# Routing one group of tiles a tile later, and giving small work to GpSimd, in a fused attention and expert kernel

## The chip, the cores and the metric

The kernel runs on one core of a Trainium2 chip. The metric is the device time of one execution in microseconds (us); lower is better. A core has five engines with instruction queues of their own: TensorE (PE in the profile; PEld is its loading of stationary operands), VectorE (DVE), ScalarE (ACT), GpSimd (POOL) and SyncE (SP), which here only issues transfers. Each queue runs in order, and engines wait for one another by semaphores. GpSimd issues the indirect transfers (scatters of rows to computed addresses).

## The reference

```python
def _attn_ref(q, k, v, omega):           # q, k, v: 8 x 8 x 576 x 64; omega: 128 x 64
    ...
    q_p, k_p = (phi(q_s), phi(k_s))      # phi: exp(h - max h) of h = x @ omega.T - |x|^2 / 2
    kv = np.einsum('bhsm,bhsd->bhmd', k_p, v)
    z = np.sum(k_p, axis=2)
    num = np.einsum('bhsm,bhmd->bhsd', q_p, kv)
    den = np.einsum('bhsm,bhm->bhs', q_p, z)[..., None] + 1e-06
    return (num / den).astype(np.float32)

def _moe_ref(x, expert_emb, tau, w1, w2):   # x: 4608 x 512, 8 experts, w1: 512 x 1024, w2: 1024 x 512
    xn = x / (np.linalg.norm(x, axis=-1, keepdims=True) + 1e-06)
    en = expert_emb / (np.linalg.norm(expert_emb, axis=-1, keepdims=True) + 1e-06)
    logits = xn @ en.T / tau
    expert_idx = np.argmax(logits, axis=1)
    ...                                      # gate_w: softmax weight of the chosen expert
    for e in range(E):
        mask = expert_idx == e
        ...
        h = np.maximum(x[mask] @ w1[e], 0.0)
        out[mask] = gate_w[mask, None] * (h @ w2[e])
    return out.astype(np.float32)
```

Linear attention with random features gives 4608 rows of 512; each row is routed to the one expert with the highest logit, and its result is weighted with the softmax weight of that expert.

## The kernel before

**Attention.** The 4608 tokens are 36 tiles of 128, nine to a pair of batch entries. One loop runs over `i` from 0 to 44. In pass `i` the key features of tile `i` are made and added into the key-value sums, and the query features of tile `iq = i - 7` (LAG is 7) are made: VectorE finds the maxima (nmk, nmq, L368), ScalarE takes the exponentials (ftk, ftq, L377), TensorE transposes (L451), ScalarE and VectorE copy (qp, L456 and L458), TensorE multiplies with the key-value sums (L471), giving `nuu` in PSUM. `num_out` (L476 to L493) divides by the denominator on VectorE, and writes the tile's row block `xr` (L490) and its logits (L486).

**Routing.** Every three tiles (a group, G is 3, 12 groups) `routed(g)` runs as a generator whose steps are put at chosen places of later passes by `plan`, with four kinds of place: `spare` and `mid` between the pieces of a pass, `ends` behind it, `behind` after the loop. Its steps: the sum of the logits over heads, on GpSimd in three operations (L510 to L512) or, for the last three groups (`fast`), on VectorE in one (L506); the maximum and the difference (L514, L515); a copy of the logits into xr on GpSimd (L518); the choice `sel` (L519 to L521); the counting of earlier rows with the same expert on TensorE (L526, L528); row numbers `base`, `pos` (L533 to L547, GpSimd, or VectorE for the last three groups); the cast of `pos` to integers `posi` on VectorE (L553); and then three scatters of the tiles' rows to `xs` in device memory, one by one (L559). For groups in `DRAINS` GpSimd's queue is drained ahead of the first scatter (L557).

**The first expert.** After group 5 (GPICK) `pick_first` (L565 to L580) chooses the expert with the most rows so far. Its weights are loaded in eight quarters from pass 29 on and split into a high and a low part: `first_split` rounds on ScalarE or VectorE, `first_rest` (L603) subtracts on GpSimd in four pieces of 128x256. From pass 36 on the generator `first_steps` gives TensorE two tiles of that expert's work between the pieces of attention, with the norms of their rows from a square root by integer and float steps (`root`, L145 and L146 on VectorE, then 13 operations on GpSimd, L148 to L156).

**Expert steps.** After the loop come the padding rows (`pad`), the table of steps, and 36 steps `t` from 2 to 37 (`ends` is 37). Each multiplies one tile of 128 rows with a pair of weight matrices, as three products of high and low parts (L280): the hidden layer, then the down product of an earlier step (`u = t - 2`). Weights come by quarters; `split` rounds them on VectorE (L230) and subtracts on GpSimd (L235) in four pieces, in one piece for the last two steps. The hidden rows are transposed by transfers on SyncE (L1050), put together on VectorE (L1062) and split (L1078, L1082). `x_of(t + 3)` loads rows into a ring of six tiles (L183), `scaled` multiplies by the gate (L287), `store` scatters the rows to the output (L310). In a step from 6 on the order is: scaling, w1 split, store, w2 split, hidden product, transposes, down product, x load of step t + 3.

**The end** (L1232 to L1250). The down product of step 36, scaling of step 35, the w2 split, the store of 35, the down product of step 37, scaling and store of step 36, one more w2 split, a DRAIN of GpSimd's queue, the last row half on ScalarE (L1247) and half on VectorE (L1248), and its store. A loop for further steps follows, which runs only when the table needs more than 38.

TensorE's and GpSimd's orders in the attention stage are as written by hand; so are VectorE's and ScalarE's in the loop.

## Time and profile before

| | |
|---|---|
| time, median of 3 runs | 646.91 us (646.56 to 648.96) |
| profiled execution: time | 647.41 us |
| its span, first to last instruction | 645.8 us |
| mean granted TensorE clock | 0.994 of full |
| TensorE busy | 627.1 us (97%) |
| VectorE busy | 498.0 us (77%) |
| ScalarE busy | 431.4 us (67%) |
| GpSimd busy | 423.7 us (66%) |

The times are of whole executions; the rows below are of the profiled one, whose span leaves 1.6 us of its time outside. The attention loop ends near 224 us, the expert steps fill the rest.

### The profile page before, as it was taken

How to read it: one execution, taken by the hardware profiler on the slowest of the kernel's cores; microseconds unless marked ns; L12 is line 12 of the kernel's file. 1: busy time of each engine (PE TensorE's matmuls, PEld its weight loads, DVE VectorE, ACT ScalarE, POOL GpSimd, SP SyncE). 2: the span in 40 equal slices, each digit the busy share in tenths (PEclk: the TensorE clock that was granted, in tenths of full speed). 3: DMA queues.
4: the chain of work that ended last, by engine and by line, in shares of the span. 5: the costliest groups of instructions: out<-in, count | busy, mean ns of one | idle time of the engine just before them, and what ended most of it. 6: DMA issues, size and time to landing. Idle time of an engine off the chain costs nothing.

```text
span 645.8 us, 19034 instructions
## 1 busy us (share of the span) xinstructions
PE 627.1 (97%) x6289; PEld 535.3 (83%) x6290; DVE 498.0 (77%) x926; ACT 431.4 (67%) x1102; POOL 423.7 (66%) x585
## 2 busy tenths in 40 slices
PE   8999999989989999999999999999999999999995
PEld 8899989988977788888888888888888888888884
DVE  4788898899889855687788787787878786878861
ACT  5898898888996426655757575757566656675630
POOL 1212343444888244668878887879897978698864
PEclk9999999999999999999999999999999999999998
DMA  7655665767862167958888888797888786879731
GB/s 250 186 166 167 207 209 180 225 199 272 289 211 101 69 214 295 261 160 247 215 220 206 231 226 211 195 246 200 223 213 233 205 216 205 227 205 219 218 103 45
DMA packets 142238, 131.92 MB, mean 204 GB/s; under 512 B 106742, under 2 KB 106870, under 8 KB 142144
## 3 DMA queue, kind: packets, MB, share of 16 engines
q1 hardware_dynamic: 135520, 109.70, 60.9%
q0 software_dynamic: 6480, 20.91, 9.4%
q8 instruction: 57, 0.93, 0.6%
q14 instruction: 37, 0.30, 0.1%
q10 hardware_dynamic: 144, 0.07, 0.0%
HBM read 83.78 MB, written 21.97 MB: 164 GB/s over the span
## 4 chain that ended last, share of the span: by engine, by line
PE 88%; ACT 4%; DVE 4%; issue 2%; POOL 1%; DMA 1%; POOLq 0%; SPq 0%; DVEq 0%; ACTq 0%
PE pb L280 31%; PE po L280 30%; PE pb L364 10%; PE kva L395 5%; PE nuu L471 5%; PE nuu L451 2%; PE fs_o L280 2%; ACT ftk L377 2%; ACT ftq L377 1%; PE pb L262 1%; PE fs_a L280 1%; DMA kt<-kT 1%; PE nuu L395 1%; DVE xr L490 1%; DVE nmq L368 1%
## 5 line engine op out<-in xcount | busy, mean ns | idle before, releaser
L235 POOL TENSOR_TENSOR w2l<-raww,w2h 128x256 f32 (+1 forms) x130 | 144.1, 1108 | 12.3 <-DVE w2h L230 3.9
L235 POOL TENSOR_TENSOR w1l<-raww,w1h 128x256 f32 (+1 forms) x130 | 122.6, 943 | 44.7 <-DVE w1h L230 34.5
L280 PE MATMUL po<-w2h,hh 128*128 (+1 forms) x288 | 112.4, 390 | 0.4 <-POOL w2l L235 0.4
L280 PE MATMUL po<-w2h,hl 128*128 (+1 forms) x288 | 112.2, 390 | 0.0
L280 PE MATMUL po<-w2l,hh 128*128 (+1 forms) x288 | 112.1, 389 | 0.0
L280 PE MATMUL pb<-w1h,xh 128*128 (+1 forms) x280 | 109.5, 391 | 0.0
L280 PE MATMUL pb<-w1h,xl 128*128 (+1 forms) x280 | 109.0, 389 | 0.0
L280 PE MATMUL pb<-w1l,xh 128*128 (+1 forms) x280 | 109.0, 389 | 0.0
L1044 DVE COPY pl<-pb 128x512 uint16<-128x512 uint16 x68 | 46.7, 689 | 60.0 <-ACT pl L1040 59.7
L377 ACT ACTIVATE ftk<-pb,nmk 128x128 f32<-128x128 f32 x288 | 80.1, 438 | 6.8 <-DVE nmk L368 6.7
L377 ACT ACTIVATE ftq<-pb,nmq 128x128 f32<-128x128 f32 x288 | 79.9, 404 | 3.3 <-DVE nmq L368 3.0
L1040 ACT ACTIVATE pl<-pb 128x512 uint16<-128x512 uint16 x68 | 39.4, 584 | 63.0 <-PE pb L280 32.9
L1062 DVE COPY wd<-t 128x1024 uint16<-128x1024 uint16 x68 | 65.8, 969 | 1.5 <-DMA t<-pl 1.5
L1078 ACT ACTIVATE hh<-wd 128x1024 fp32r<-128x1024 f32 x34 | 36.1, 1062 | 45.6 <-DVE wd L1062 40.0
L280 PEld LDWEIGHTS po<-w2h,hh 128*128 128x128 f32 x288 | 54.1, 188 | 11.9 <-POOL w2l L235 0.8
L280 PEld LDWEIGHTS po<-w2h,hl 128*128 128x128 f32 x288 | 54.0, 188 | 11.6 <-DVE hl L1082 0.3
L280 PEld LDWEIGHTS po<-w2l,hh 128*128 128x128 f32 x288 | 54.0, 187 | 11.2
L280 PEld LDWEIGHTS pb<-w1l,xh 128*128 128x128 f32 x280 | 52.7, 188 | 10.9
L280 PEld LDWEIGHTS pb<-w1h,xl 128*128 128x128 f32 x280 | 52.6, 188 | 11.0
L280 PEld LDWEIGHTS pb<-w1h,xh 128*128 128x128 f32 x280 | 52.5, 187 | 10.7
L1082 DVE SCALAR_TENSOR_TENSOR hl<-wd,hh 128x1024 fp32r<-128x1024 f32 x34 | 55.2, 1622 | 6.6 <-ACT hh L1078 6.2
L559 POOL DMA_INDIRECT xs<-xr,posi x36 | 36.4, 1012 | 28.5 <-DVE qp L458 8.2
(333 smaller groups left out, 1242.5 us busy)
## 6 DMA issues: line engine op xcount, KB each, us to landing
raww<-w1q SPq DMA_DIRECT2D x38, 512.0 KB, 4.0
raww<-w2q SPq DMA_DIRECT2D x38, 512.0 KB, 4.8
kt<-kT SPq DMA_DIRECT2D x36, 256.0 KB, 3.7
qt<-qT SPq DMA_DIRECT2D x36, 256.0 KB, 3.5
xgp<-xs SPq DMA_DIRECT2D x20, 260.5 KB, 2.8
xg<-xs SPq DMA_DIRECT2D x18, 260.5 KB, 2.7
rf<-w1q SPq DMA_DIRECT2D x4, 512.0 KB, 3.6
rf<-w2q SPq DMA_DIRECT2D x4, 512.0 KB, 5.6
```

Source lines behind the costliest of these rows:

```text
L235: ils.append(nc.gpsimd.tensor_tensor(at(l, dp)[:, c], raw[:, c], at(h, dp)[:, c].bitcast(F32), op=ALU.subtract))
L280: done.append(nc.tensor.matmul(dst, x[:, c * P : (c + 1) * P], ws.rearrange("p o f -> p (o f)"), start=(begin and i == 0 and k == 0), stop ...
L364: nc.tensor.matmul(st["pj" + w, i, a][:, c, :], st[w, i][r, c, :], om[r, :], start=True, stop=True)
L377: nc.scalar.activation(ft[:, h, :], pj[:, h, :], AF.Exp, bias=nm[:, h : h + 1])
L395: nc.tensor.matmul(acc[c : c + 64, h, :], ft[:, h, c : c + 64], vt[:, 2 * h + a, :], start=begin and h == 0, stop=u == 4 + 4 * b and h == 3,)
L471: nc.tensor.matmul(pn[a][s * D : s * D + D, h, :], st["qp", i, s][:, 2 * h + a, :], kvs[sb, int(u > 4 - s)][:, 4 * a + h, :], start=True, ...
L559: w = nc.gpsimd.indirect_dma_start(out=xs, out_offset=bass.IndirectOffsetOnAxis(ap=posi[:, j : j + 1], axis=0), in_=xr, in_offset=None, bo ...
L1040: nc.scalar.activation(planes[1][:, o : o + 512], halved(src)[:, :, 1], AF.Copy)
L1044: nc.vector.tensor_copy(planes[0][:, o : o + 512], halved(src)[:, :, 0])
L1062: nc.vector.tensor_copy(to, src)
L1078: nc.scalar.activation(hh, wd[:, 0:F], AF.Relu)
L1082: nc.vector.scalar_tensor_tensor(hl, wd[:, 0:F], 0.0, hh.bitcast(F32), op0=ALU.max, op1=ALU.subtract)
```

## The change

- `posi` is cast on GpSimd for groups 0 to 8, on VectorE for the last three as before.
- `pick_first` makes three operations on VectorE and ten on GpSimd, with a constant `pickc` made at the start.
- The root for the first expert's rows is asked for after three columns of its first product in place of before the first.
- Group 10 (the last but one) sums its logits on GpSimd, and its steps are placed about a pass later.
- Each scatter waits for the latest `num_out`, and the scatters of groups 8 and 9 are placed a pass later, one a pass.
- DRAINs at groups 10 and 11 and at step NQ go; new ones stand before the pads, after the first expert's work and in the last step. Those at groups 3 and 6 wait for the latest `num_out`.
- In the expert steps the store stands ahead of the w1 split, and from step 6 on the x load of step t + 3 ahead of the hidden product.
- At the end the w2 splits of the last two steps are subtracted on VectorE, the first of them ahead of the scaling, and the last row is scaled on ScalarE in one piece.

```diff
-DRAINS = (3, 6, 10, 11)
+DRAINS = (3, 6)
...
+    pickc = const.tile([P, E], F32, name="pickc")
+    nc.gpsimd.tensor_scalar(pickc, iote, -float(REG * E + 1), 0.0, op0=ALU.mult, op1=ALU.add)
...
             piece = F if t is None or t >= NSTAT - 2 else PIECE
+            eng, d = (nc.vector, dv) if wn == "w2" and t is not None and t >= NSTAT - 2 else (nc.gpsimd, dp)
             for c in range(0, F, piece):
                 c = slice(c, c + piece)
-                ils.append(nc.gpsimd.tensor_tensor(at(l, dp)[:, c], raw[:, c], at(h, dp)[:, c].bitcast(F32), op=ALU.subtract))
+                ils.append(eng.tensor_tensor(at(l, d)[:, c], raw[:, c], at(h, d)[:, c].bitcast(F32), op=ALU.subtract))
...
-            nc.vector.tensor_tensor(
+            st["out"] = nc.vector.tensor_tensor(
                 xr[:, 0:DM].rearrange("p (h a d) -> p a h d", a=2, d=D),
...
-            if fast:
+            pt = nc.gpsimd.tensor_tensor
+            if fast and g != NTILE // G - 2:
                 nc.vector.tensor_reduce(raw, lg.rearrange("p g h e -> p g e h"), axis=AX.X, op=ALU.add)
...
-            nc.vector.tensor_copy(posi, pos[:, :, 0])
+            (nc.vector if fast else nc.gpsimd).tensor_copy(posi, pos[:, :, 0])
             for j in range(G):
                 yield
                 if j == 0 and g in DRAINS:
-                    nc.gpsimd.drain()
+                    tc.add_manual_dep(nc.gpsimd.drain().ins, st["out"].ins.name, sync, reason="idle behind the last scatter")
...
+                tc.add_manual_dep(w.ins, st["out"].ins.name, sync, reason="one scatter a tile")
                 written(w)
...
         def pick_first():

+            pt, ts = nc.gpsimd.tensor_tensor, nc.gpsimd.tensor_scalar
             cnt = small.tile([P, E], F32, name="cnt0", tag="cnt")
-            nc.vector.scalar_tensor_tensor(cnt, iote, -float(REG), run, op0=ALU.mult, op1=ALU.add)
             m = small.tile([P, 1], F32, name="m0", tag="m0")
+            nc.vector.scalar_tensor_tensor(cnt, run, float(E), pickc, op0=ALU.mult, op1=ALU.add)
             nc.vector.tensor_reduce(m, cnt, axis=AX.X, op=ALU.max)
-            nc.vector.tensor_scalar(cnt, cnt, m, None, op0=ALU.is_ge)
-            nc.vector.tensor_tensor(cnt, cnt, iotm, op=ALU.mult)
-            nc.vector.tensor_reduce(m, cnt, axis=AX.X, op=ALU.min)
+            nc.vector.tensor_scalar(isf, cnt, m, None, op0=ALU.is_ge)
             yield
-            nc.vector.tensor_scalar(first, m, float(E), None, op0=ALU.add)
+            pt(cnt, isf, iote, op=ALU.mult)
+            pt(cnt[:, 0:4], cnt[:, 0:4], cnt[:, 4:8], op=ALU.add)
+            pt(cnt[:, 0:2], cnt[:, 0:2], cnt[:, 2:4], op=ALU.add)
+            pt(first, cnt[:, 0:1], cnt[:, 1:2], op=ALU.add)
             for t in range(NPRE + 1):
-                nc.vector.tensor_scalar(firsti[:, t : t + 1], first, float(REG), float(t * P), op0=ALU.mult, op1=ALU.add)
-            nc.vector.tensor_copy(firsti[:, NPRE + 1 :], first)
-            nc.vector.tensor_scalar(isf, iote, first, None, op0=ALU.is_equal)
-            nc.vector.scalar_tensor_tensor(keyc, isf, float(2 * E * N), iote, op0=ALU.mult, op1=ALU.subtract)
+                ts(firsti[:, t : t + 1], first, float(REG), float(t * P), op0=ALU.mult, op1=ALU.add)
+            nc.gpsimd.tensor_copy(firsti[:, NPRE + 1 :], first)
+            ts(keyc, isf, float(2 * E * N), 0.0, op0=ALU.mult, op1=ALU.add)
+            pt(keyc, keyc, iote, op=ALU.subtract)
...
+            pa = new("a00", "kv0")
+            yield from up(0, 0, range(3), pa)
             nrm = root(gp, n2, NPRE, "p", nc.gpsimd)
-            yield from up(0, 0, range(4), new("a00", "kv0"))
+            yield from up(0, 0, [3], pa)
...
+                elif g == NTILE // G - 2:
+                    plan = [(ends, i), (ends, i + 1), (ends, i + 1), (spare, i + 2, 0), (mid, i + 2, 0), (mid, i + 2, 1)]
+                    plan += [(ends, i + 2), (ends, i + 3), (ends, i + 3)]
                 elif i >= NTILE:
                     plan = [(ends, i)] * 3 + [(spare, i + 1, 0), (mid, i + 1, 0), (mid, i + 1, 1)]
-                    plan += [(ends, i + 1 + k) for k in range(3)]
+                    plan += [(ends, i + 2 + k) for k in range(3)]
...
                 if NTILE - 3 < i < NTILE:
-                    plan[-3:] = [(ends, i + 3), (ends, i + 3), (mid, i + 4, 3)]
+                    plan[-3:] = [(ends, i + 3), (mid, i + 4, 3), (ends, i + 5)]
...
         x2 = got.pop()
+        nc.gpsimd.drain()
         for e in range(1, PADP):
             pad(e)
...
         for _ in fill:
             flush()
+        nc.gpsimd.drain()
...
-                for v in po:
+                for v in list(po):
                     scaled(po[v], xg[v], gates[v])
-            if t == NQ:
-                nc.gpsimd.drain()
+                    store(v, xg[v])
+                    po.pop(v)
             if t not in (NPRE + 1, ends):
                 split("w1", t if t > NPRE else 0)
             if t > SHIFT:
-                for v in list(po):
-                    po.pop(v)
-                    store(v, xg[v])
                 split("w2", u)
                 if t == ends:
                     split("w1", t)
+                    nc.gpsimd.drain()
+                elif t + 3 < NSTAT:
+                    xg[t + 3] = x_of(t + 3, reg("row", t + 3))
...
-            if t + 3 < NSTAT:
+            if t <= SHIFT:
                 xg[t + 3] = x_of(t + 3, reg("row", t + 3))
...
         v = ends - 2
+        split("w2", ends - 1)
         scaled(po.pop(v), xg[v], gates[v])
-        split("w2", ends - 1)
         store(v, xg[v])
...
         nc.gpsimd.drain()
-        last = po.pop(ends)
-        nc.scalar.activation(xg[ends][:, DM // 2 : DM], last[:, DM // 2 :], AF.Copy, scale=gates[ends])
-        nc.vector.tensor_scalar(xg[ends][:, 0 : DM // 2], last[:, 0 : DM // 2], gates[ends], None, op0=ALU.mult)
+        nc.scalar.activation(xg[ends][:, 0:DM], po.pop(ends), AF.Copy, scale=gates[ends])
         store(ends, xg[ends])
```

## Rows read from the trace of the kernel before

**Rows 1.** The page's engine totals: busy us (share of the span) and instructions.

```profile
PE 627.1 (97%) x6289; PEld 535.3 (83%) x6290; DVE 498.0 (77%) x926; ACT 431.4 (67%) x1102; POOL 423.7 (66%) x585
```

**Rows 2.** Table of windows, whole core: stretch, busy time of each engine, PEclk, DMA.

```profile
180.00:195.00 15.00, 13.87 (x267) 11.78 (x262) 11.53 (x29) 14.62 (x46) 13.31 (x29) 1.00 0.56 186
...
270.00:620.00 350.00, 350.00 (x1551) 289.75 (x1550) 275.71 (x370) 217.06 (x409) 288.79 (x283) 1.00 0.80 214
```

**Rows 3.** Waits of TensorE, 130 to 270 us: total us, times, longest.

```profile
PE nuu L451 <- DVE first L575: 1.4, 1, 1.4
PE nuu L451 <- DVE xr L490: 1.4, 1, 1.4
PE nuu L526 <- DVE sel L521: 1.1, 2, 0.7
...
PE nuu L451 <- DVE kvs L439: 0.7, 1, 0.7
```

**Rows 4.** Table of windows around the low clock, same columns.

```profile
160.60:164.00 3.40, 3.40 (x50) 3.17 (x46) 2.93 (x6) 2.67 (x9) 2.37 (x5) 0.50 0.92 272
```

**Rows 5.** Timeline of VectorE: start us, us, line, operation, shapes.

```profile
156.92 2.20 DVE L553 CAST posi<-pos 128x3 int32<-128x3 f32 x1
...
176.52 1.74 DVE L553 CAST posi<-pos 128x3 int32<-128x3 f32 x1
```

**Rows 6.** Timeline of VectorE beside the pick.

```profile
142.69 0.16 DVE L553 CAST posi<-pos 128x3 int32<-128x3 f32 x1
```

**Rows 7.** Timeline of GpSimd beside the first cast of rows 5.

```profile
156.92 2.78 POOL L603 TENSOR_TENSOR w1l<-rf,w1h 128x256 fp32r<-128x256 f32 x4
```

**Rows 8.** Timelines of GpSimd (root, 13 operations, first and last) and VectorE.

```profile
202.06 0.20 POOL L148 TENSOR_TENSOR rtt_p<-n2p,rt_p 128x2 f32<-128x2 f32 x1
...
205.40 0.20 POOL L156 TENSOR_TENSOR rt_p<-rt_p,n2p 128x2 f32<-128x2 f32 x1
...
211.34 0.49 DVE L506 TENSOR_REDUCE raw<-lg 128x24 f32<-128x192 f32 x1
...
212.87 1.27 DVE L368 TENSOR_REDUCE nmq<-pb 128x4 f32<-128x512 f32 x2
```

**Rows 9.** Timeline of GpSimd beside the pick of the first expert.

```profile
143.13 0.99 POOL L559 DMA_INDIRECT xs<-xr,posi  x1 [3.43 <-DVE posi L553]
```

**Rows 10.** Timelines of the end; sources of DRAINs, L1082, L456 (ns min/median/max).

```profile
630.59 2.39 POOL L235 TENSOR_TENSOR w2l<-raww,w2h 128x1024 f32 x1 [3.92 <-DVE w2h L230]
...
641.65 0.99 POOL L310 DMA_INDIRECT y<-xgp  x1 [3.82 <-issue]
...
633.03 0.50 PE L280 MATMUL po<-w2h,hh 128*128 x1 [0.41 <-POOL w2l L235]
...
638.90 0.47 ACT L1247 ACTIVATE xgp<-po,totalb 128x256 f32<-128x256 f32 x1 [11.04 <-PE po L280]
...
L1245 POOLq DRAIN  x1: 6544/6544/6544, 634.2 to 634.2; - x1
...
L557 POOLq DRAIN  x4: 1099/2791/4789, 105.7 to 222.9; - x4
...
L1082 DVE SCALAR_TENSOR_TENSOR hl<-wd,hh x34: 1216/1654/2203, 264.6 to 619.9; 128x1024 fp32r<-128x1024 f32 x34
...
L456 ACT ACTIVATE qp<-nuu x28: 597/598/744, 30.2 to 180.4; 128x512 f32<-128x512 f32 x28
```

**Rows 11.** Timelines of one steady step; landings of L310 (first), L1050.

```profile
611.36 2.65 SPq L1050 DMA_TRANSPOSE t<-pl  x2
...
605.71 0.74 DVE L287 TENSOR_SCALAR xg<-po,totalb 128x512 f32<-128x512 f32 x1
...
608.53 2.02 DVE L1062 COPY wd<-t 128x1024 uint16<-128x1024 uint16 x1
...
DMA to landing us min/median/max: 2.6/3.2/5.2
...
DMA to landing us min/median/max: 2.8/3.5/5.3
```

More of the change, by code (lines that the diff above doesn't have):

```diff
@@ L504, in routed @@
             fast = g >= NTILE // G - 3
-            if fast:
+            pt = nc.gpsimd.tensor_tensor
+            if fast and g != NTILE // G - 2:
                 nc.vector.tensor_reduce(raw, lg.rearrange("p g h e -> p g e h"), axis=AX.X, op=ALU.add)
             else:
-                pt = nc.gpsimd.tensor_tensor
                 t4 = new("t4", [P, G, 4, E])
```

## The prediction

> **What bounds the kernel now.** I read the page's engine totals first: TensorE is busy for 627.1 of 645.8 us [rows 1], so only some 19 us can be had without taking work from it. The table of windows says where they are. From 270 to 620 us, the steady expert steps, TensorE is busy for all of 350.00 us at full clock [rows 2]; nothing done to the other engines can gain a microsecond there, only lose. What is left is the attention stage from 140 to 224 us and the last 16 us.
>
> In the attention stage the waits of TensorE name VectorE each time: 1.4 us on the normalised row xr (L490), 1.4 us beside the choice of the first expert (L575), 1.1 us in two waits on sel (L521) and 0.7 us on kvs (L439) [rows 3]. Behind the first stands a second loss: from 160.60 to 164.00 us TensorE is busy without a break, but the granted clock is 0.50 [rows 4], the lower of its two levels, and this starts right where the 1.4 us gap ended. The 1.4 us gap beside the pick was not followed by such a drop, so one gap of this length does not always bring it.
>
> Why VectorE was late at L490 is in its timeline. The cast posi (L553, 128x3) took 2.20 us from 156.92 on [rows 5]; the same cast takes 0.16 us at 142.69 [rows 6]. In the same stretch GpSimd ran the four subtractions of L603, which started at the same 156.92 [rows 7]. It happened once more: 1.74 us at 176.52 [rows 5], ahead of the 0.7 us wait on kvs.
>
> **The positions on GpSimd (nine of twelve).** The cast leaves VectorE for groups 0 to 8 and runs on GpSimd, in line ahead of its own scatter; a GpSimd operation on such small tiles has a row at 0.20 us [rows 8]. Being on the same engine as L603 it can't collide with it. For the group at 156.92 this takes 2.0 us off the chain to L490, more than the 1.4 us gap. With the gap I let the low clock go: 3.40 us at half speed hold 1.70 us of full-clock work, so up to 1.7 us come back; I take 1.5, since VectorE and ScalarE may have limited some of that stretch anyway. Together 2.9 us (bounds 1.4, if the clock drops all the same, and 3.1). At 176.52 the stall was 1.6 us and the gap 0.7 us: I take 0.7 (0 to 0.7).
>
> The page "SBUF — State Buffer" of the Trainium skill, section "SBUF: two separate sides", says that VectorE and GpSimd share a pair of ports as an exclusive lock, held for the whole instruction, and that a VectorE operation in a two-port mode waits until the holder has finished. One piece of L603 takes 2.78/4 = 0.70 us [rows 7], so one wait would be 0.7 us and the gap at L490 would not have come about; by that this term would be near 0.5 us instead of 2.9. The row shows 2.20, the time of three pieces, and the row decides: the cast got in only after several.
>
> **The pick on GpSimd.** Ahead of num_out two small VectorE operations go (with their spacing some 0.2 us each, as the cast's 0.16), and behind it six more and the cast itself, over at 142.85 [rows 6]. The gap of 1.4 us there ended as VectorE came to L575, the operation right behind num_out, so 0.4 us of it goes, and I give 0.3 us for the seven behind it: 0.7 us (0 to 1.4, the whole gap). On GpSimd ten operations at 0.28 us apart, as the 13 of the root run [rows 8], make 2.8 us; GpSimd had idled for 3.43 us just there [rows 9], so they are hidden; without that cover the scatter behind them and the sums of the next group come up to 2.8 us later.
>
> **Root, last group but one, scatters.** The square root goes from the tile around 198 us to that around 211 us. Its two VectorE operations then no longer stand in front of sel, where TensorE waited 1.1 us in two waits [rows 3]; the larger of these, 0.7 us, I take as gone (0 to 1.1). At 211.34 the routing of the last group but one keeps VectorE until 212.87 [rows 8], ahead of nmq; that is 1.5 us; its being a tile later, with the sums on GpSimd, I credit with half, 0.8 us, since TensorE has other work beside it. Against it stands GpSimd's new work in that tile: root 3.5 us [rows 8], a scatter 0.99 [rows 9], the sums some 0.9 (three at 0.28 apart at least), 5.4 us in one tile. VectorE's norms and the group's maximum can then wait 1 to 2 us a tile later. I take 0.4 (−1.0 to 0.8). The extra waits of each scatter for the latest num_out hold up what is queued behind on GpSimd, the subtractions of L603 and the sums; they follow VectorE's work by tile as now, so I price them at nothing, with the loss kept in the second rival.
>
> These five are 2.9 + 0.7 + 0.7 + 0.7 + 0.4 = 5.4 us. ScalarE is busy for 14.62 of 15 us between 180 and 195 [rows 2], so time won before can't all be kept through there; I take a fifth off: 4.3 us.
>
> **DRAINs.** Those at groups 10 and 11 go, and three come: ahead of the pads, behind the first expert's steps, and in the last step. The pads wait for an x load anyway, and the last step's DRAIN lies behind GpSimd's last split of that step, with an idle GpSimd after it. The four DRAINs at groups took 1.1 to 4.8 us, mostly beside idle [rows 10]. Zero.
>
> **Steady steps.** The store now precedes the w1 split on GpSimd, and the x load precedes the step's transposes on SyncE. With TensorE full [rows 2] there is nothing to win. It loses only if it makes a step late; see the last rival. Zero.
>
> **The end.** TensorE's last product waits for GpSimd's low part: the subtraction 128x1024 took 2.39 us from 630.59, and the first product came at 633.03 after 0.41 us of idle [rows 10]. On VectorE the nearest operation with two SBUF inputs of this size has a median of 1.65 us [rows 10]. Its cast no longer stands behind a scaling, so it does not start later than 630.59 and ends by 632.3, before the products are ready to go. The products come 0.65 us sooner: the 0.41, and an estimated 0.24 for the product's longer run (that row has 0.50 us) and the overlap with the product before it that a filled pipeline has. Then the last row: ScalarE started at 638.90 its half (0.47 us), VectorE did the other after it, and the store started only at 641.65 [rows 10], because the DRAIN in front of it ran from 634.2 for 6.54 us, to 640.78 [rows 10]. GpSimd's subtraction (2.4 us) ran under that DRAIN; it is now on VectorE, and the earlier DRAIN leaves only two stores to wait for. So I expect it over before the result is there. ScalarE's whole 128x512 row costs 0.60 us (the median of L456 [rows 10]), and a scatter started 0.28 us after its input (142.85 to 143.13 [rows 6, 9]). 638.25 + 0.60 + 0.28 = 639.13 against 641.65: 2.5 us. If the DRAIN is as long again, it starts some 0.7 us earlier and the gain is 0.75 us.
>
> **Sum.** 4.3 + 2.5 = 6.8 us off the profiled execution's 647.41 us: 640.6. The median of the three runs is 646.91, 0.5 us below; I say 640.4 us.
>
> **Rivals.**
> *The DRAIN at the end stays 6.5 us long.* For it: nothing shows what a DRAIN waits for. Against: the group ones were shorter [rows 10]. 4.3 + 0.75: 642.2 us.
>
> *GpSimd, or ScalarE, becomes late in the attention stage.* GpSimd is busy 13.31 of 15 us between 180 and 195 [rows 2], and gets positions, the scatters' waits, and 5.4 us of work in one tile around 211. If half the 4.3 us goes to that, the time is 642.6; if a further microsecond or two, 643.5 to 644.5. The Trainium skill's "GPSIMD Engine Reference", section "Engine selection", speaks for this one: it sends elementwise work on tiles to VectorE and puts GpSimd at about half its speed. The rows agree in direction (0.20 us there against 0.16).
>
> *The stall only moves.* Another VectorE operation comes to stand beside L603 where the cast stood, and waits as long: then the change does not do what it says for the two big stalls. 0.8 x (2.9 + 0.7) = 2.9 us are missing: 643.3 us. The Trainium skill's page "SBUF — State Buffer", section "Who interferes with whom", names copies and casts as operations that can wait so. Against: TensorE's waits name none of them there [rows 3].
>
> *Slower: the x load holds up the transposes.* The ring has six tiles, so step t's load of x(t+3) waits until the store of step t−3 has landed, which is issued in the same step. SyncE now waits for that ahead of the transposes. Today they are issued from 611.36 in the step whose scaling (L287) runs from 605.71 to 606.45 [rows 11]. A store issued behind that, near 606.6, lands 2.6 to 5.2 us later (median 3.2) [rows 11], at 609.2 to 611.8; with 0.35 us for the load the transposes go at 612.2 at worst, 0.8 us late. The two transposes take 2.65 us to issue, so the later one starts near 612.7 and lands 2.8 to 5.3 us after, by 618.0 at worst; it is first used in the next step, which by L1062 at 608.53 in this one is near 619.4 [rows 11]. That leaves 1.4 us at the worst landing. So it decides only when stores land over 5.8 us after they are issued, by a GpSimd held up beside VectorE's casts, say. Every 0.4 us beyond that costs 0.4 us in each of 33 steps, 13 us: about 653.
>
> **Chances.** Forecast 0.50 (638 to 642); long DRAIN 0.13; late GpSimd or ScalarE 0.22, half of it above 643.7; the stall moves 0.08, likewise half; slower 0.07. Half a per cent, 3.2 us, is what a measurement here can tell from no change, so the bound is 643.7. Faster: 0.50 + 0.13 + 0.11 + 0.04 = 0.78; within: 0.11 + 0.04 = 0.15; slower 0.07. The range: from 637.5 (nothing absorbed, 5.4, and the upper bounds of pick and sel, 1.0, with 3.0 at the end, from the median) to 644.8 (1.4 us for the first gap alone and 0.75 at the end): outside are the slow case and a few per cent at either end.
>
> **What would show it.** No VectorE operation of about 2 us near 157 and 177; no wait of 1.4 us on xr; the granted clock at 1.00 throughout 150 to 165; no wait of TensorE in the last 20 us, ScalarE's last row at 0.60 us and the last store within 0.4 us of its end; windows of the steady steps still full. It is wrong if TensorE waits for GpSimd from 195 on, if the clock falls elsewhere, if the last store still waits for its DRAIN, or if a steady step shows a wait on hl or w1l.

## The result and the profile after

The changed kernel took 652.79 us in the median of 8 executions (651.02 to 655.65), the kernel before 647.43 us on the same chip (8 executions, 646.11 to 649.05): a ratio of 1.0082 (95% interval 1.0062 to 1.0102). It is slower by 5 us; the prediction had it faster by 6.5. The profiled execution of the changed kernel took 653.73 us, its span is 652.1 us, 6.3 more than before. Line numbers are 2 to 6 higher than before in the attention stage (L490 is now L493, L603 is L609) and mostly 12 or 13 higher in the expert steps.

The page's engine totals, which answer to [rows 1]:

```profile
PE 629.3 (97%) x6289; PEld 535.5 (82%) x6290; DVE 483.3 (74%) x908; ACT 429.8 (66%) x1102; POOL 405.7 (62%) x606
```

TensorE is busy 2.2 us longer with the same 6289 instructions; the other 4.1 us are new idle time. The table of windows (stretch, busy time of the engines, granted clock, DMA) says where:

```profile
150.00:165.00 15.00, 14.73 (x336) 13.76 (x336) 13.96 (x31) 13.34 (x47) 7.71 (x16) 1.00 0.83 307
165.00:180.00 15.00, 12.47 (x288) 11.44 (x284) 11.23 (x27) 13.41 (x46) 13.80 (x30) 1.00 0.87 265
...
210.00:224.00 14.00, 11.38 (x175) 9.34 (x176) 9.25 (x33) 6.42 (x20) 7.37 (x25) 0.88 0.16 60
270.00:620.00 350.00, 347.36 (x1531) 285.32 (x1529) 262.21 (x364) 216.10 (x413) 271.64 (x283) 1.00 0.85 214
...
68.80:72.20 3.40, 3.40 (x47) 3.17 (x47) 2.89 (x5) 3.31 (x12) 1.32 (x3) 0.50 0.31 107
219.00:222.40 3.40, 3.09 (x38) 2.85 (x39) 2.50 (x13) 0.00 (x0) 1.76 (x7) 0.50 0.28 103
```

The first row is what was hoped for: 14.73 us busy at full clock, where the kernel before has 13.64 at 0.89. The low clock of [rows 4] is gone from there (though the same kernel run again, below, has none there either). But it stands at two new places, 68.8 and 219.0 (and once more in the first 11 us); the windows from 165 and from 210 lost 1.8 and 1.5 us of busy time (14.23 and 12.84 before); and the steady stretch, full in [rows 2], lacks 2.64 us. TensorE's waits over the whole span (total us, times, longest) name the causes, beside [rows 3]:

```profile
PE nuu L454 <- DVE xr L493: 3.5, 3, 1.9
PE pb L367 <- DMA kt<-kT: 3.1, 2, 1.6
PE nuu L474 <- DVE xr L493: 2.1, 1, 2.1
PE pb L283 <- DVE xl L1094: 2.0, 2, 1.4
...
PE po L283 <- DVE hl L1095: 0.5, 1, 0.5
```

Taken tile by tile, the start of L493 (`num_out` writing `xr`) in the changed kernel less that of L490 in the one before, its delay, shows five parts. At tiles 6 and 7 the delay jumps from −0.1 to +3.6 us; at the pick (tile 20) it falls to 2.6 and by tile 23, where the cast's stall was, to 0.4; by tile 26 it is up at 1.7; from tile 32 to 35 it grows from 1.1 to 4.2; and TensorE's last product starts 8.1 us later than before, against 4.8 us later at the first scaling of the expert steps. These are differences of two single executions, and two executions of one kernel differ too, as the control below shows. By them the attention terms came, some 3 us, and more than that was lost before, behind and after them.

**First loss: the first scatter.** Timelines of GpSimd, VectorE and TensorE, and the queue instructions of the scatters' line:

```profile
57.05 0.19 POOL L556 CAST posi<-pos 128x3 int32<-128x3 f32 x1
57.18 0.19 POOL L482 COPY xr<-ids 128x1 int32<-128x1 int32 x1
64.11 1.26 POOL L562 DMA_INDIRECT xs<-xr,posi  x1 [6.75 <-DVE nmk L371]
65.40 0.40 POOL L513 TENSOR_TENSOR t<-lg 128x96 f32<-128x96 f32 x1
...
59.49 0.68 DVE L493 TENSOR_TENSOR xr<-nuu,rr 128x512 f32<-128x512 f32 x1
...
66.52 0.18 DVE L517 TENSOR_REDUCE mx<-raw 128x3 f32<-128x24 f32 x1 [3.05 <-POOL raw L515]
...
68.14 0.71 PE L454 MATMUL nuu<-ident,ftq 64*128 64x64 f32 x16 [1.91 <-DVE xr L493]
...
L562 POOLq EVENT_SEMAPHORE  x13: 17/17/17, 60.2 to 229.7; - x13
```

The scatter's `num_out` (L493) was over at 60.17 and the queue's wait for it at 60.22, yet the scatter started only at 64.11, 3.89 us later. The releaser named in the row (nmk) ended 0.65 us ahead of it, in two of the runs below 0.75 and 1.06 us ahead, so it doesn't look like the cause. The group's sums stand behind the scatter, VectorE waited 3.05 us for them, and TensorE 1.91 us for the next `xr`; right behind that the clock fell. Later scatters behind such a wait start 0.74 us after it (one, whose positions came later still, 2.93 us after).

**Second loss: the logits' single buffer.** The same engines at the last group but one:

```profile
216.22 0.20 POOL L158 TENSOR_TENSOR rt_p<-rt_p,n2p 128x2 f32<-128x2 f32 x1
216.95 1.02 POOL L562 DMA_INDIRECT xs<-xr,posi  x1 [0.53 <-issue]
217.99 0.41 POOL L513 TENSOR_TENSOR t<-lg 128x96 f32<-128x96 f32 x1
...
215.30 0.20 DVE L488 RECIPROCAL rr<-rr 128x8 f32<-128x8 f32 x1
218.43 0.23 DVE L489 TENSOR_TENSOR lg<-nuu,rr 128x64 f32<-128x64 f32 x1 [2.93 <-POOL t L513]
...
219.31 2.21 PE L474 MATMUL nuu<-kvs,qp 128*64 128x73 f32 x32 [2.14 <-DVE xr L493]
```

`lg` holds one group. The first `num_out` of the next group overwrites it (L489), and GpSimd had still to read it: it made the root first, then a scatter, and read `lg` from 217.99. VectorE stood for 2.93 us in the middle of `num_out`, TensorE for 2.14, and the clock fell as it went on.

**Third loss: a key tile.** TensorE waited for its load at 175.81; the loads are SyncE's; the scatter is that of group 6, now and before:

```profile
175.81 1.16 PE L367 MATMUL pb<-om,kt 64*128 64x128 f32 x16 [1.58 <-DMA kt<-kT]
...
169.20 0.34 SPq L594 DMA_DIRECT2D rf<-w2q  x1
169.67 1.19 SPq L338 DMA_DIRECT2D kt<-kT  x1
...
164.32 1.00 POOL L562 DMA_INDIRECT xs<-xr,posi  x1 [1.67 <-DVE nmk L371]
...
161.45 1.00 POOL L559 DMA_INDIRECT xs<-xr,posi  x1 [1.62 <-DVE w2h L596]
```

In SyncE's queue the key tile stands behind a weight quarter (L594), which waits for its buffer, and that comes free when GpSimd has subtracted. The weight load went 2.87 us later than before (166.33), since GpSimd was behind. The DRAIN at group 6, which waits for `num_out` now and lasted from 160.72 to 163.45, is hardly a part of that: GpSimd stood 1.67 us in front of this scatter, 1.62 before. It came to this group's subtractions 2.16 us late already (159.08 against 156.92), with the delay of the first loss, and they took 3.31 us in place of 2.78. VectorE had made most of that delay good by tile 23, GpSimd had not; so VectorE waited 1.65 us for the sums behind this scatter, and TensorE 0.95 us for `xr`, a tile later.

**Fourth loss: steady steps.** Landing times of the stores (L313) and transposes (L1063), who waited for the transposes, and SyncE's waits at the x load, beside [rows 11]:

```profile
DMA to landing us min/median/max: 2.8/5.7/7.0
...
DMA to landing us min/median/max: 3.1/4.1/5.9
...
  ACT pl L1053: 86.2, 31
...
SPq L185 <- DMA y<-xgp: 67.1, 15, 6.1
```

The stores go out among the weight loads now and land in 5.7 us, not 3.2; SyncE stands up to 6.1 us at an x load that waits for them, the transposes behind it.

**The gain: the end.** GpSimd, ScalarE, TensorE and the last DRAIN, beside [rows 10]:

```profile
647.95 0.97 POOL L313 DMA_INDIRECT y<-xgp  x1 [4.25 <-ACT xgp L1259]
...
646.99 0.69 ACT L1259 ACTIVATE xgp<-po,totalb 128x512 f32<-128x512 f32 x1 [10.29 <-PE po L283]
...
646.51 0.39 PE L283 MATMUL po<-w2h,hl 128*128 x1
...
L1258 POOLq DRAIN  x1: 3137/3137/3137, 642.3 to 642.3; - x1
```

The DRAIN was over at 645.43, before the result. From the last product's start to the last store are 1.44 us, 3.23 before (638.42 to 641.65), and no product waits for a low part.

### The profile page after: what moved, and what is told of

Same layout as the page of the kernel before. It is cut to its first block, busy times and chain, and to the rows that moved or that the text cites. A ratio compares the mean times of both kernels' runs of the same rounds, so it can differ in the third digit from the quotient of the medians.

```text
span 652.1 us, 19088 instructions
## 1 busy us (share of the span) xinstructions
PE 629.3 (97%) x6289; PEld 535.5 (82%) x6290; DVE 483.3 (74%) x908; ACT 429.8 (66%) x1102; POOL 405.7 (62%) x606
## 4 chain that ended last, share of the span: by engine, by line
PE 32%; DMA 22%; ACT 22%; DVE 15%; issue 4%; POOL 2%; SPq 1%; POOLq 1%; ACTq 0%; DVEq 0%
DMA t<-pl 19%; PE pb L367 9%; ACT pl L1053 7%; ACT wd L1077 6%; PE po L283 5%; PE nuu L474 5%; PE kva L398 4%; DVE wd L1075 4%; PE pb L283 3%; DVE pl L1057 3%; ACT hh L1091 3%; ACT pl L1055 2%; PE nuu L454 2%; DMA kt<-kT 2%; DVE xl L1094 1%
## 5 line engine op out<-in xcount | busy, mean ns | idle before, releaser
L238 POOL TENSOR_TENSOR w2l<-raww,w2h 128x256 f32 x128 | 130.3, 1018 | 7.6
L238 POOL TENSOR_TENSOR w1l<-raww,w1h 128x256 f32 (+1 forms) x130 | 112.8, 867 | 14.6 <-DVE w1h L232 6.4
L1075 DVE COPY wd<-t 128x1024 uint16<-128x1024 uint16 x68 | 64.0, 942 | 2.3 <-DMA t<-pl 2.3
L283 PEld LDWEIGHTS pb<-w1l,xh 128*128 128x128 f32 x280 | 52.6, 188 | 10.9
```

What stands on the lines that cost most here:

```text
L238: ils.append(eng.tensor_tensor(at(l, d)[:, c], raw[:, c], at(h, d)[:, c].bitcast(F32), op=ALU.subtract))
L283: done.append(nc.tensor.matmul(dst, x[:, c * P : (c + 1) * P], ws.rearrange("p o f -> p (o f)"), start=(begin and i == 0 and k == 0), stop ...
L1075: nc.vector.tensor_copy(to, src)
```

## The experiments

Medians of the kernel before lay at 646.8 to 652.8 us on the chips of these runs, so only ratios to the kernel before on the same chip are compared, with 95% intervals. My theory: the four losses are separate, each tied to one edit, and undoing it gives its price back (the first to the scatters' wait, the second to the late group, the third to the DRAINs' wait, the fourth to the x load). Rivals: the x load costs it all; the low clock strikes where it will, and the stalls do no harm by themselves; or the edits do harm only together.

**Undoing one edit of the changed kernel.** The scatters' wait for `num_out` goes:

```diff
-                tc.add_manual_dep(w.ins, st["out"].ins.name, sync, reason="one scatter a tile")
```

> The changed kernel with one part undone: a scatter no longer waits for the latest num_out. In the changed kernel the first scatter of the program started 3.9 us after that wait ended (64.11 against 60.22), held the sums behind it on GpSimd, made VectorE idle for 3.05 us and TensorE for 1.91 us, and the clock fell for 3.41 us after that. Theory: the wait makes this stall, so without it some 3.5 us come back, about 649.3 us, with no half clock near 69. Rival: the first scatter costs this wherever it stands behind an idle GpSimd, then it stays near 652.8 us with the same gap.

1.0035 (1.001 to 1.006). No gap and no low clock near 67; the 2.1 us gap on `xr` near 217 stays, here without a low clock behind it, and the window from 270 to 620 is busy for 345.90 us, less than the 347.36 of the changed kernel. The x load goes back to the end of the step:

```diff
-                elif t + 3 < NSTAT:
-                    xg[t + 3] = x_of(t + 3, reg("row", t + 3))
-            if t <= SHIFT:
+            if t + 3 < NSTAT:
```

> The changed kernel with the x load of step t + 3 back at the end of the step, the store still ahead of the w1 split. Theory: the x load at the head of SyncE's queue waits for the step's own store, which now lands 5.7 us (median) after issue because the step's two weight loads are ahead of it, and the transposes queue behind the load; with the load back, TensorE's waits of 0.46, 0.64 and 1.40 us in the steady steps go: 2.5 to 3.9 us less, about 649.5 us. Rival: the early store itself, landing among the weight loads, slows the transposes; then the waits stay and the time is near 652.5 us.

1.0022 (0.9997 to 1.0047); one steady wait is left (1.21 us), though the stores land as late (6.3 us median). The root and the last group but one go back:

```diff
-            if fast and g != NTILE // G - 2:
+            if fast:
...
-            yield from up(0, 0, range(3), pa)
-            yield from up(0, 0, [3], pa)
+            yield from up(0, 0, range(4), new("a00", "kv0"))
...
-                elif g == NTILE // G - 2:
```

> The changed kernel with the root and the routing of the last group but one back in their old places and the sums of that group back on VectorE. Theory: root, a scatter and the sums, 5.4 us of GpSimd in one tile, keep the logits buffer of that group, which num_out of the next tile overwrites: VectorE waits 2.93 us, TensorE 2.14, and the clock falls for 3.41 us. Undone, 3.1 us less by TensorE's delay there, and the old gaps of about 1.5 us come back: about 651 us, no half clock near 220. Rival: VectorE is late there anyway by the later scatters: near 652.8 us, with a gap that names xr again.

0.9994 (0.9977 to 1.0012), more than the 1.6 us that were expected to come back; no gap on `xr` near 219 and no low clock there. The first scatter is late again in this run and in the one before it, 4.00 and 4.30 us behind the wait. Each of the three is worth 0.5 to 0.9% against 1.0082 (which is from another chip). All three undone:

> All three parts undone at once: no wait of the scatters for num_out, the x load at the end of the step, root and last group but one as before. Left of the change: positions and pick on GpSimd, scatters a pass later, store ahead of the w1 split, DRAINs, and the new end. If the three losses are separate and the gains forecast are real: 652.8 - 3.5 - 3.2 - 1.6 = 644.5 us, 0.4 per cent below the kernel before. If the gains never came: 647 us.

0.9939 (0.9909 to 0.9969), and the window from 270 to 620 is full again. The x load alone therefore isn't the cause. With the group DRAINs also freed of their wait for `num_out`:

```diff
-                    tc.add_manual_dep(nc.gpsimd.drain().ins, st["out"].ins.name, sync, reason="idle behind the last scatter")
+                    nc.gpsimd.drain()
```

> The changed kernel with the three parts undone (scatters' wait, early x load, root and last group but one) and also the wait of the two DRAINs for num_out. Theory: the DRAINs that start only behind num_out hold GpSimd 1.5 to 3 us longer; the subtractions of the first expert's weights come later, SyncE waits for their buffers ahead of the key tiles, and TensorE waited 1.45 us for a key tile and 1.23 us on xr in the run with three undone. Without it some 2.5 us less than that run: a ratio to the kernel before of 0.990. Rival: the key tile is late by SyncE's other loads, then 0.994 as that run.

0.9956 (0.993 to 0.9982): no more. The wait for a key tile is not tied to this edit either. It stands at the same place in three runs told further down whose DRAINs are those of before (the control, the scatters' wait alone, the late group alone):

```profile
172.88 1.16 PE L364 MATMUL pb<-om,kt 64*128 64x128 f32 x16 [0.97 <-DMA kt<-kT]
...
171.75 1.16 PE L364 MATMUL pb<-om,kt 64*128 64x128 f32 x16 [1.53 <-DMA kt<-kT]
...
174.29 1.53 PE L364 MATMUL pb<-om,kt 64*128 64x128 f32 x16 [2.21 <-DMA kt<-kT]
```

It is missing where the scatters' wait or the early x load alone is undone, with the DRAINs' wait in place. In the three runs that have it the cast near 157 took at most 1.43 us and tile 23 followed tile 22 sooner by 0.8 to 1.4 us than in the trace of [rows 5], so the key tile may be the next limit behind the stall on `xr`; that is not shown. Then the changed kernel with the wait from the second group on:

```diff
-                tc.add_manual_dep(w.ins, st["out"].ins.name, sync, reason="one scatter a tile")
+                if g > 0:
+                    tc.add_manual_dep(w.ins, st["out"].ins.name, sync, reason="one scatter a tile")
```

> The changed kernel with the scatters' wait for num_out taken from the first group alone. If the 3.9 us belong to the first scatter of the program when it stands behind a wait of GpSimd's queue, the second group's scatter, now the first that waits so, starts 0.74 us after its wait ends, and there is no gap of 1.9 us near 67 us. If they belong to the first scatter that waits so, the stall moves to the second group, near 81 us. The gap near 219 us stays in either case.

1.0017 (0.9991 to 1.0042), and no stall at the second group, where the first waiting scatter now is. The 3.9 us belong to the program's first scatter; why it takes them is open.

**One edit alone in the kernel before.** The control, the same kernel again:

> The kernel before once more, for its profile on the chip of the other three runs of this call. Expected: its own time, and its gaps of 1.4 us beside the pick and at 160 us.

0.9994 (0.9975 to 1.0013); its casts L553 took 1.43 and 1.22 us, its low clock fell at 204.0. So the stall and the place of the low clock change between executions of one kernel. Its delay against the trace of [rows 1], as above, goes from −1.2 us at tile 0 to +5.7 at tile 35 (the median is 5 us higher on this chip); a difference of two traces is evidence only where its cause stands in the rows. The scatters' wait alone:

```diff
-            nc.vector.tensor_tensor(
+            st["out"] = nc.vector.tensor_tensor(
...
+                tc.add_manual_dep(w.ins, st["out"].ins.name, sync, reason="one scatter a tile")
```

> The kernel before with one edit: each scatter waits for the latest num_out. Theory: the first scatter starts late behind this wait, GpSimd's sums come late, VectorE and TensorE wait near 65 us and the clock falls: 2 to 3.5 us more, a ratio of 1.004. Rival: the wait costs this only where the positions are made on GpSimd, since the scatter then waits for two engines; here it waits for VectorE alone: 1.000, no gap near 65 us.

0.9991 (0.997 to 1.0012). GpSimd's timeline has the first scatter 0.31 us behind its `num_out`, which ends at 58.71 here:

```profile
59.02 1.25 POOL L559 DMA_INDIRECT xs<-xr,posi  x1 [3.37 <-DVE xr L490]
```

Here the rival was right: the wait is harmless while the cast comes from VectorE, and costs some 3 us with the cast on GpSimd. With one engine to wait for, the scatter carries its wait itself; in the changed kernel it waits for GpSimd's cast and a queue instruction in front of it for VectorE. Root and last group but one alone:

```diff
-            if fast:
+            if fast and g != NTILE // G - 2:
...
-            yield from up(0, 0, range(4), new("a00", "kv0"))
+            yield from up(0, 0, range(3), pa)
+            yield from up(0, 0, [3], pa)
```

> The kernel before with one part: the root after three columns, and the last group but one routed a tile later with its sums on GpSimd. Theory: the logits buffer of that group is read late by GpSimd, VectorE's num_out of the next tile waits some 2.5 us, TensorE 2 us, the clock may fall: 1.5 to 3 us more, less the old gaps of 0.8 us there: a ratio of 1.003. Rival: only the later scatters make GpSimd late, 1.000.

1.0061 (1.0039 to 1.0082), 4 us by itself. Timelines of VectorE and TensorE, and a window:

```profile
218.81 0.23 DVE L486 TENSOR_TENSOR lg<-nuu,rr 128x64 f32<-128x64 f32 x1 [2.93 <-POOL t L510]
...
219.69 2.22 PE L471 MATMUL nuu<-kvs,qp 128*64 128x73 f32 x32 [2.15 <-DVE xr L490]
...
219.30:222.70 3.40, 3.01 (x38) 2.77 (x39) 2.50 (x12) 0.00 (x0) 0.88 (x6) 0.50 0.13 44
```

The same wait and gap to 0.01 us, with no other edit in it. The gap (2.15) and the half of 3.01 us at half speed (1.5) make 3.65 of the 4 us in this execution. The new order of the steady steps alone:

```diff
+                    store(v, xg[v])
+                    po.pop(v)
...
+                elif t + 3 < NSTAT:
+                    xg[t + 3] = x_of(t + 3, reg("row", t + 3))
```

> The kernel before with the new order of the steady steps alone: store ahead of the w1 split, x load ahead of the hidden product and so of the transposes. Theory: the store lands 5.5 us or more after issue, SyncE holds the transposes behind the x load until then, VectorE's xl comes 1 us later in each step, with no slack left, and TensorE waits several times for xl: 2 to 4 us more, a ratio of 1.004. Rival: the waits in the changed kernel came of its other parts, 1.000.

0.9997 (0.998 to 1.0014). Landing of its stores, and the steady window:

```profile
DMA to landing us min/median/max: 2.6/5.3/6.7
...
270.00:620.00 350.00, 350.00 (x1551) 289.78 (x1550) 270.68 (x371) 215.73 (x409) 275.77 (x283) 1.00 0.81 215
```

The stores land late here too, and TensorE never waits: again the rival that an edit alone is harmless. The new end alone, and with the last step's DRAIN too (its one more line is `nc.gpsimd.drain()` behind that step's w1 split):

```diff
+            eng, d = (nc.vector, dv) if wn == "w2" and t is not None and t >= NSTAT - 2 else (nc.gpsimd, dp)
...
-        nc.scalar.activation(xg[ends][:, DM // 2 : DM], last[:, DM // 2 :], AF.Copy, scale=gates[ends])
-        nc.vector.tensor_scalar(xg[ends][:, 0 : DM // 2], last[:, 0 : DM // 2], gates[ends], None, op0=ALU.mult)
+        nc.scalar.activation(xg[ends][:, 0:DM], po.pop(ends), AF.Copy, scale=gates[ends])
```

> The kernel before with the new end alone: the w2 splits of the last two steps on VectorE, the first ahead of the scaling, the last row on ScalarE in one piece; the DRAIN stays the only one after the pads. Theory, as predicted: 2.5 us less, a ratio of 0.9961. Rival: the one DRAIN behind all stores lasts 6.5 us again and the last store waits for it, 0.75 us less, a ratio of 0.9988; then the gain in the changed kernel comes from the DRAIN put into the last step.

> The kernel before with the new end and the DRAIN in the last step. Theory: the last store follows ScalarE within 0.4 us, 2.5 to 3.3 us less, a ratio of 0.9955. Rival: as in the run with the new end, positions and pick, the steady steps lose it again by waits on xl: 1.000 or above.

0.9949 (0.9931 to 0.9968) and 0.9969 (0.9947 to 0.9991), 3.3 and 2.0 us. From the last product's start to the last store are 1.43 and 1.44 us in the two traces, as in the changed kernel, so the DRAIN in the last step adds nothing: without it the one DRAIN took 4.49 us and was over before the last row, and the rival of 6.5 us is out. Perhaps not all of the 3.3 us is the end: the two traces have no low clock ahead of the last product, the control's has one. The granted clock as a mean over all executions (0.9986 and 0.9975, against 0.9947 and 0.9965 of the kernel before beside them) can't be turned into time here, because it also counts the stretch behind the last product, with TensorE idle at 0.50: 3.9 us of it in the kernel before (from 641.9 on), 0.6 and 1.7 us in these two traces.

**The positions.** Alone in the kernel before:

```diff
-            nc.vector.tensor_copy(posi, pos[:, :, 0])
+            (nc.vector if fast else nc.gpsimd).tensor_copy(posi, pos[:, :, 0])
```

> The kernel before with one edit: the positions of groups 0 to 8 are cast on GpSimd. Theory, as predicted: the casts of 2.20 and 1.74 us go from VectorE, the wait of 1.4 us on xr and the half clock at 160 us with them, and the wait of 0.7 us on kvs: 2.9 + 0.7 = 3.6 us less, a ratio of 0.9945. Rival, the stall only moves to another VectorE operation: less than 1 us, a ratio above 0.9985.

1.0005 (0.9989 to 1.0021). The window from 150 to 165 is busy for 14.95 us (14.12 in the control), as predicted; but TensorE's timeline, and the window of 180 to 195 (13.51 in the control), show in the profiled execution:

```profile
189.56 0.48 PE L451 MATMUL pb<-ident,ftq 64*128 64x64 f32 x5 [2.68 <-issue]
...
180.00:195.00 15.00, 11.92 (x210) 10.52 (x207) 9.38 (x22) 11.03 (x34) 12.76 (x29) 0.79 0.62 210
```

That gap waits for nothing that the profile shows, and from 188.6 to 195.4 the clock is 0.50. This execution is the slowest of its twelve (655.36 us, the median is 653.16), so the gap explains it and not the median. To see the edit without the weight loads beside it I cut these to a sixteenth; in this pair the first expert's weights are read from 64 columns, which are used again for the others:

```diff
-            nc.sync.dma_start(raw, W[wn][0].rearrange("(e q) p f -> e q p f", q=NQ)[ds(st["fe"], 1), q].rearrange("o p f -> (o p) f"))
+            nc.sync.dma_start(raw[:, 0:64], W[wn][0].rearrange("(e q) p f -> e q p f", q=NQ)[ds(st["fe"], 1), q, :, 0:64].rearrange("o p f -> (o p) f"))
```

> The kernel before with the eight loads of the first expert's weights cut to a sixteenth: 64 columns are loaded and read over and over in place of 1024, so the first expert's products are of other weights; the arithmetic is as much as before. It is one half of a pair. Where transfers set the stage from 160 to 190 us, this alone takes away the waits on key tiles and the waits of TensorE that name no releaser near 186 us, some 1 to 2 us: a ratio of 0.998; where they don't, 1.000.

> The other half: the same light loads, and the positions of groups 0 to 8 cast on GpSimd. Theory: with all loads the casts on GpSimd gained nothing, since what VectorE won was waited out again on key tiles and on TensorE's own instructions, which come by the same transfer engines as the weights; with light loads it is kept, 2 to 3 us less than the other half, a ratio of 0.994. Rival: casts on GpSimd win nothing in themselves, VectorE or ScalarE takes the time elsewhere: both halves equal within 0.1 per cent.

0.9995 (0.9975 to 1.0015) and 0.9992 (0.997 to 1.0013): still nothing from the edit. GpSimd and VectorE of the second one:

```profile
160.14 0.18 POOL L479 COPY xr<-ids 128x1 int32<-128x1 int32 x1
161.95 0.99 POOL L559 DMA_INDIRECT xs<-xr,posi  x1 [1.62 <-issue]
...
163.81 0.24 POOL L512 TENSOR_TENSOR raw<-t 128x24 f32<-128x24 f32 x1
...
157.72 0.68 DVE L490 TENSOR_TENSOR xr<-nuu,rr 128x512 f32<-128x512 f32 x1
...
164.08 0.18 DVE L514 TENSOR_REDUCE mx<-raw 128x3 f32<-128x24 f32 x1 [1.60 <-POOL raw L512]
```

`xr` is written at 157.72 (159.60 before, [rows 5] being in its way), and a tile later VectorE waits 1.60 us for GpSimd's sums: 164.08, against 164.35 before. The 1.62 us of GpSimd ahead of its scatter are the DRAIN at group 6. So I took that DRAIN out, without and with the edit:

```diff
-DRAINS = (3, 6, 10, 11)
+DRAINS = (3, 10, 11)
```

> The kernel before without the DRAIN ahead of group 6's first scatter, the control of a pair. The cast of 2.2 us on VectorE and the wait of 1.4 us on xr stay, since they come of L603; the scatter and the sums behind it come up to 1.5 us earlier, for nobody. Expected 1.000.

> The same, with the positions of groups 0 to 8 cast on GpSimd. Theory: with the DRAIN, what VectorE wins at 157 us it waits out a tile later for GpSimd's sums (L512), which stand behind the scatter and the DRAIN; without it the sums end near 162.5 in place of 164.1, the wait of 1.6 us at L514 and the gap of 0.9 us at 166 are gone, and the gain is kept to the next tiles: 1 to 2 us below the control by the num_out of tile 25, a ratio of 0.998. Rival: the next limit, a key tile or ScalarE, stands right behind, and the time equals the control's, 1.000.

1.0034 (1.0009 to 1.0059), slower than the 1.000 expected, and 0.9977 (0.9955 to 0.9999). With the edit:

```profile
160.62 1.00 POOL L559 DMA_INDIRECT xs<-xr,posi  x1 [0.16 <-POOL xr L479]
...
162.76 0.18 DVE L514 TENSOR_REDUCE mx<-raw 128x3 f32<-128x24 f32 x1
```

No wait on the sums is left, and the edit is worth 3.6 us between the medians (654.49 and 650.87), but only 1.9 us against the kernel before beside them (652.80); why the control is slower is open. By the mean clocks, 0.9939 and 0.9966, an estimated 1.8 us of the 3.6 lie in the clock: the control's trace has a low clock from 202.6 to 206.0, the other's none. Whether the edit keeps the clock up or these executions had luck is not settled.

**A better kernel.** Before with the new end, the positions and the pick:

> What the runs so far speak for: the kernel before with the new end, positions and pick on GpSimd, and nothing else of the change. The end alone gave 0.9949. Theory: the pick takes another 0.5 to 0.9 us away beside 142 us, part of which is waited out later: 0.994. Rival: all of it is waited out, 0.995 as the end alone.

1.0058 (1.0033 to 1.0082), not the 0.994 expected. Its attention stage ends 1.4 us earlier than before, and with the old order of the steady steps TensorE then waits in them (its waits, beside a window of 346.96 busy in 350):

```profile
PE pb L283 <- DVE xl L1086: 2.8, 7, 0.7
```

## Why the prediction was wrong

**Root, last group but one: the step that failed most.** I priced GpSimd's 5.4 us of new work as VectorE's norms and maximum waiting "1 to 2 us a tile later", and came to a gain of 0.4 with −1.0 as the bound. Measured alone it loses 4 us. The late-GpSimd rival had the place, around 211, and the right engine, but the price was wrong: what waits is `num_out` itself, because its logits tile has one buffer that GpSimd reads, and the low clock behind the gap nearly doubled it in the profiled execution.

**The scatters' waits: priced at nothing.** In the changed kernel this step cost 3.1 us by undoing it (1.0082 to 1.0035). I had named what is queued behind the scatters, the sums, assumed that a wait that has ended costs no more, and kept the loss in the second rival, near 180 and 211 us. The 3.89 us behind it (4.00 and 4.30 in two more runs) show otherwise for the first scatter near 60 us, and only with the positions on GpSimd: two edits that I priced apart.

**Positions, 3.6 us: right where it looked, given back where it did not.** The casts take 0.19 us, the gap and the low clock are gone from 150 to 165, and the delay falls by 1.8 us at tile 23. Alone the edit is worth nothing (1.0005): the sums on GpSimd, behind DRAIN and scatter, are next in line 0.3 us below the old time. I had allowed for the next limit only with a fifth off the sum, and for ScalarE. The rival that the stall only moves came true in a form it did not have: the time went to GpSimd's queue, not to another VectorE operation. The 1.5 us for the clock had the right size (in four versions without that low clock tile 24 follows tile 23 sooner by 1.5 to 1.6 us), but they were not the edit's to give back: gaps of the same size at the same place (1.33 to 1.38 us in the order run, both runs of the end and the light control) were not followed by a low clock there; in the order run and in three controls it fell near 203 instead. By the page "SBUF — State Buffer" of the Trainium skill, section "SBUF: two separate sides", a VectorE operation in a two-port mode waits until the GpSimd instruction that holds the ports is over; one instruction takes 0.70 us here [rows 7]. Casts of 1.22 and 1.43 us in the control, 2.20 and 1.74 in [rows 5], agree with a wait, but with one of one to three pieces; the trace doesn't show the mode.

**Pick and sel, 1.4 us.** The delay falls by 0.8 at tile 20 and by 0.4 at tile 21 in the changed kernel; with the positions alone it falls by 0.4 at tile 20 only, so about 0.8 us are the pick's, where 0.7 was said. TensorE's waits on `sel` are 0.4 us, 1.1 before; the same kernel run again has 2.4, so that says little. Neither was timed alone.

**DRAINs, priced at nothing: not shown wrong.** I took the 1.58 us of TensorE on a key tile for the price of the DRAIN at group 6. Freeing it, once the other three were undone, gave nothing, GpSimd stood as long in front of that scatter as before, and runs with the old DRAINs show the same wait.

**Steady order, priced at nothing; the slower rival.** I put the decisive point at a landing of 5.8 us. The stores now reach 7.0, since I took their landing from the old place in the step. Alone the order still costs nothing, as the prediction said. In the changed kernel 2.64 us are lost there and moving the x load back gave 0.6%. But over the traces with the early x load the window lacks 0 to 4.10 us (0 alone, 1.36 with the first group's waits off, 4.10 with all off), and the last combination lost 3 us there with the old order and stores that land in 3.0 us. So neither the order nor the landing is the whole cause; what makes some versions wait for `xl` stays open. The slower rival's "about 653" meets the measured time by luck: its mechanism was to cost 13 us in this window.

**The end, 2.5 us: right.** The trace has 1.8 us from the last product on and the 0.41 us of waiting gone; measured alone it is 2.0 to 3.3 us, the upper figure perhaps with a low clock less. ScalarE's row took 0.69 us, 0.60 was said. The long-DRAIN rival is out (3.14 us).

Forecast and loss put together by prices of the runs: −2.0 to −3.3 for the end, about 0 for the positions, +4 for the late group, +3 for the first scatter, +2.6 for the steady steps are +6 to +8 us, where the measured loss is 5.4. They overlap (undone one by one the three parts give 2.0% in all, together 1.4%), and each has an uncertainty of about 1.5 us. One slip of the sum itself: 640.6 less the 0.5 us between profiled execution and median is 640.1, not 640.4.

## What to carry to other kernels

When small work moves to an engine with slack on average, look up for each tile that it reads how many buffers there are and who writes it next: the wait shows at that writer, not at the reader's result. Price edits that touch one queue together, at the first instruction that both of them reach. And a stall that is removed is worth only the distance to the next limit: here 1.9 us were won at one tile and 1.6 us of it went to the next engine's queue a tile later.

## What the runs showed that was not expected

- The program's first scatter, behind a wait of its queue and with its positions from GpSimd, started 3.89, 4.00 and 4.30 us after the wait ended in three runs; later ones 0.74 us.
- Indirect stores landed in 3.2 us (median) at the old place of the step and in 5.3 to 6.3 us among the weight loads.
- The same DRAIN instruction took 1.04 us to 6.80 us at different places of the changed kernel.
- TensorE stood 2.68 us with nothing released (positions alone, 189.56). A packet of an instruction queue (q8) lies in that stretch, from 187.2 to 188.2, 10.9 us behind the one before it. Gaps of 0.72 to 1.86 us that name no releaser end at the same product in four other runs. That a late packet makes them is not shown.
- The granted clock fell to 0.50 behind gaps of TensorE of 0.8 to 2.6 us in some executions, and in others it didn't behind gaps of 1.3 to 2.3 us: at 160.6 in the kernel before, at 204.0 in the same kernel run again, at 202.4 to 203.0 in three versions of it.
